# A 2D spectral filter and a 32-head attention on one core: earlier first tiles of x, fewer warming matmuls, a tail with narrow reciprocals, and other settings of the static order

## The chip, the core and the metric

The kernel runs on one core of a Trainium2 chip. The metric is the device time of one execution in microseconds (us). Several executions of a kernel are timed, each kernel beside the kernel before on the same chip; all executions quoted here were in the fast state. The profile is one of these executions, recorded. It has a "span", from its first to its last counted instruction, and the time of the same execution, which is somewhat longer. Two instants are used throughout: **F**, the start of the first softmax exponential on ScalarE, and **E**, the end of the last one. Head is what lies before F, tail what lies after E.

## The reference, cut to what matters

```python
def _A_ref(x, w_r, w_i):            # x: 1 x 2048 x 640
    X = rfft2(x.astype(float32)); X = X * (w_r + 1j * w_i)
    return irfft2(X, s=(2048, 640)).astype(bfloat16)
def _B_ref(x, wqkv, wo):            # 32 heads of 20, S = 2048, D = 640
    q, k, v = split_heads(x @ wqkv)
    p = softmax(q @ k.T * 20 ** -0.5)
    return merge_heads(p @ v) @ wo
return concatenate([a, b], axis=-1) # 1 x 2048 x 1280
```

Part A is computed with matmuls against Fourier matrices. Part B has 32 x 16 x 4 = 2048 score tiles of 128 x 512, each of which must be exponentiated.

## The kernel before: the parts concerned

The program is a generator. A scheduler runs on the host with estimated durations (`occupy`, `self.now`), decides which operation each engine does next and so writes one fixed order of instructions for each engine. The chip then follows these orders and waits only at semaphores. A change of an estimate or of a setting therefore changes the order for the whole run.

ScalarE exponentiates most score tiles, in groups of three and two PSUM banks; VectorE does 234 of the tiles with a polynomial.

```python
def try_exp(self):                                  # L1751
    ...
    self.P.add("act", lambda e: e.activation(pt, in_, AF.Exp, scale=SCALE, bias=-15.0 / LOG2E), ...)
    t = self.occupy("act", 512 * n * 0.8333 + 50.0, 0.0)
```

The head loads constants, then the first quarter of x (640 KB) as one transfer, all on SyncE's queue, and lets TensorE do 24 dummy matmuls to raise its clock.

```python
def setup_B(self):
    self.dma(self.ident, cBd.ap(), ...)
    self.dma(self.kq, kqd.ap(), ...)
    ldx(0); ldw(640, 736, "k0"); ldq(0, 96, 0); ldx(1); ldw(1280, 1360, "v0"); ldx(2); ldx(3)
    ...
    P.add("dve", lambda e: e.memset(ws, 0.25), ...)            # operand of the dummies
for i in range(cfg["WARMUP"]):                                 # 24
    self.dummy(i % 6)
```

The tail is the output projection of the last 512 rows. The row sums of the last unit are spread by a matmul to 128 x 512, inverted in four reciprocals of 128 x 128, and meanwhile TensorE does 28 pairs of output matmuls for the first seven head groups (`# ...` marks cuts).

```python
def tail_pe(self):
    ...
    self.P.add("pe", lambda e: e.matmul(ps[:, 5, :], sel, osb, start=True, stop=True), ...)   # L2040
    for qb in range(4):
        self.dve_urgent.append((self.tail_b, lambda qb=qb: self.tail_norm(qb)))
def tail_norm(self, qb):
    self.P.add("dve", lambda e: e.reciprocal(rb, b), ...)                                     # L2060
    self.P.add("dve", lambda e: e.tensor_tensor(o, osb, rb, ALU.mult), ...)
def tail_act(self):
    self.P.add("act", lambda e: e.copy(o[:, 0:512], ps[:, qb, :]), ...)                       # L2078
    self.P.add("act", lambda e: e.copy(o[:, 512:640], ps[:, 4, qb * 128:(qb + 1) * 128]), ...)
    self.P.add("sp", lambda e: e.dma_start(dst, o), ...)
```

The end of the program matters for what follows. A certificate is computed from the largest values met (reductions, three comparisons, a matmul that sums them, a comparison: `emit_flag`). Then every engine loads the verdict and branches over a second, slower program that would redo attention exactly.

```python
def run_engine(ename):
    def body(eng):
        fast.engine_body(fs, ename, eng)
        eng.wait_ge(fs["s_" + flag_task.eng], flag_task.count)     # wait for the verdict
        bad = eng.value_load(flag, min_val=0, max_val=3)
        with eng.If(bad > 0):
            ...
            slow.engine_body(ss, ename, eng)                       # a whole second program
        if ename == "sp": ...                                      # wait for the last stores
```

Of the kernel before, what the change touches and what calls it, by code (L numbers as in the profile page):

```python
# [10 lines left out]
BF16 = mybir.dt.bfloat16  # L11
U16 = mybir.dt.uint16
AF = mybir.ActivationFunctionType
# [1371 lines left out]
class FK(KB):  # L1385
# [8 lines left out]
    def alloc(self):  # L1394
# [21 lines left out]
        self.ws = a.bf(b0, 656)  # L1416
# [13 lines left out]
        self.ones1 = a.f32(take(32), 8)  # L1430
        self.zt = self.ones1.bitcast(BF16)[:, 8:9]
        self.sel = a.f32(take(512), 128)
# [3 lines left out]
    def zone(self, z, total):  # L1436
# [21 lines left out]
        self.ZT = a.bf(zC, 3 * 16 * 2 * 128).rearrange("p (t s c a) -> p t s c a", t=3, s=16, c=2)  # L1458
        self.yA = a.bf(zA, 16 * 640).rearrange("p (s d) -> p s d", s=16)
# [6 lines left out]
    def setup_B(self):  # L1466
        P = self.P
        cBd = self.inline(f32_to_bf16_bits(np.eye(128, dtype=np.float32)), "ident")
        self.dma(self.ident, cBd.ap(), w=[("ident",)], name="ld_ident")
# [5 lines left out]
        self.dma(self.kq, kqd.ap(), w=[("kq",)], name="ld_kq")  # L1475
# [3 lines left out]
        def ldx(i):  # L1479
            self.dma(self.xBn[:, 4 * i:4 * i + 4, :], xB[:, 4 * i:4 * i + 4, :], w=[("xBn", i)], name="ld_xB%d" % i)  # L1480
# [6 lines left out]
        ldx(0)  # L1487
        ldw(640, 736, "k0")
        ldq(0, 96, 0)
        ldx(1)  # L1490
        ldw(1280, 1360, "v0")
        ldx(2)
        ldx(3)
        ldw(736, 1280, "k")
        ldq(96, 640, 1)
        ldw(1360, 1920, "v")
        wq, ws, zt, va, ps, o1 = self.wq, self.ws, self.zt, self.Vaug, self.ps, self.ones1
        wo = self.wo_pad.rearrange("p g n -> p (g n)")
        P.add("dve", lambda e: e.memset(ws, 0.25), w=[("ws",), ("xa", 0)], name="ms_ws")
        P.add("act", lambda e: e.activation(ws[:, 640:648], ws[:, 0:8], AF.Exp), r=[("ws",), ("xa", 0)], w=[("ws2",)], name="act_warm")  # L1500
# [4 lines left out]
        P.add("dve", lambda e: e.memset(wo, 0.0), w=[("woz",)], name="ms_wo")  # L1505
# [9 lines left out]

    def load_wo(self):
        sel = np.zeros((128, 128), np.float32)
        for j in range(4):
            sel[32 * j + 20, 32 * j:32 * j + 32] = 1.0
        seld = self.nc.inline_tensor(sel, self.prefix + "sel")  # L1520
        self.dma(self.sel, seld.ap(), w=[("sel",)], name="ld_sel")
        wod = self.B_wo.rearrange("(g j d) n -> j d g n", g=8, j=4)
        for j in range(4):
            self.dma(self.wo_pad[32 * j:32 * j + 20, :, :], wod[j], r=[("woz",)], pw=[("wo",)], name="ld_wo%d" % j)
# [5 lines left out]
    def mk_jobs_B_static(self):  # L1530
        jobs = KB.mk_jobs_B_static(self)
        ps = self.ps
        for i in range(4):
            for gi in range(3):
                jobs[("xT", i, gi)].minp = (8000.0, 9500.0, 11500.0, 13000.0)[i]
        for g in range(NG):
            for kc in range(4):
# [16 lines left out]
                J.pe = pe  # L1554

# [3 lines left out]
                J.ev = [(mkev, 490.0, 600.0, [("kq",)], [("KT", g, kc)], [])]  # L1559
                J.mode = "c"  # L1560
                if g:
                    J.minp = 18500.0 + 1100.0 * g
        V = {}
        for part, h0, nh, per in ((0, 0, 4, 4), (1, 4, 4, 4), (2, 8, 12, 2), (3, 20, 12, 2)):
            n = 20 * nh
            for k0 in range(0, 16, per):
# [17 lines left out]
                J = Job("V%d_%d" % (k0, part), 0.0, pe, ev, after=[jobs[("xT", k0 // 4, gi)] for gi in range(3)], minp=19000.0 if part else 12000.0)  # L1584
# [8 lines left out]
    def dummy(self, bank, n=512):  # L1593
        ps = self.ps
        l = self.ws[:, 0:128]
        r_ = self.ident if n == 128 else self.ws[:, 128:128 + n]
        self.P.add("pe", lambda e: e.matmul(ps[:, bank, 0:n], l, r_, start=True, stop=True),
                   r=[("ws",), ("xa", 0)], w=[("ps", bank)], name="dummy")
# [19 lines left out]
    def job_QA(self, u):  # L1618
# [16 lines left out]
        def mkev(bank):  # L1635
            o = self.QA[u % 2]
            return lambda e, en: self.add_row(e, en, o, ps[:, bank, :], 2)
        ev = [(mkev, 490.0, 600.0, [("kq",)], [("QA", u % 2)], [])]
        cond = (lambda p: self.qk_left[u - 2] == 0) if u >= 2 else None
        J = Job("QA%d" % u, 0.0, pe, ev, after=[self.sj[("xT", qc, gi)] for gi in range(3)], cond=cond,  # L1640
                minp=(0.0 if u == 0 else 21000.0))
# [20 lines left out]
    def pe_dur(self, dur, mode, tiles=0):  # L1662
# [9 lines left out]
        if self.now < 12000.0:  # L1672
            dur *= 2.0
# [68 lines left out]
    def try_exp(self):  # L1742
# [10 lines left out]
        t = self.occupy("act", 512 * n * 0.8333 + 50.0, 0.0)  # L1753
# [221 lines left out]
    def unit_norm(self, u):  # L1975
# [7 lines left out]
        if u == 30:  # L1983
            self.tail_op = [(qb, g) for qb in range(4) for g in range(NG - 1)]
# [36 lines left out]
    def tail_mm(self, qb, g):  # L2021
        ps = self.ps
        l = self.OTn[:, g, qb * 128:(qb + 1) * 128]
        w1, w2 = self.wo_pad[:, g, 0:512], self.wo_pad[:, g, 512:640]

        def fn(e):
            e.matmul(ps[:, qb, :], l, w1, start=(g == 0), stop=(g == NG - 1))
            return e.matmul(ps[:, 4, qb * 128:(qb + 1) * 128], l, w2, start=(g == 0 and qb == 0), stop=(g == NG - 1),
                            skip_group_check=True)
        okey = ("OT", g) if g < NG - 1 else ("OTl", qb)  # L2030
        first = {"w": [("ps", qb)] + ([("ps", 4)] if qb == 0 else []), "pw": ([("ps", 4)] if qb else [])} if g == 0 else {"pw": [("ps", qb), ("ps", 4)]}
        self.P.add("pe", fn, r=[okey, ("wo",), ("woz",)], name="tail_op", **first)
        return self.occupy("pe", self.pe_dur(270.0, "f"), PE_LAT)

    def tail_pe(self):
        if not self.all_exp() or max(self.half_free) > self.now:
            return False
        if self.tail_t is not None and self.tail_t <= self.now and self.tail_b is None:
            ps, sel, osb = self.ps, self.sel, self.osb
            self.P.add("pe", lambda e: e.matmul(ps[:, 5, :], sel, osb, start=True, stop=True), r=[("osb",), ("sel",)], w=[("ps", 5)], name="tail_sum")  # L2040
            self.tail_b = self.occupy("pe", self.pe_dur(860.0, "f"), PE_LAT)
            for qb in range(4):
                self.dve_urgent.append((self.tail_b, lambda qb=qb: self.tail_norm(qb)))
            return True
        if self.tail_op:
            qb, g = self.tail_op.pop(0)
            self.tail_mm(qb, g)
            return True
        for qb in range(4):
            if self.tail_n.get(qb, 1e18) <= self.now:  # L2050
                del self.tail_n[qb]
                t = self.tail_mm(qb, NG - 1)
                self.tail_ev.append((t, qb))
                return True
        return False

    def tail_norm(self, qb):
        c = slice(qb * 128, (qb + 1) * 128)
        rb, b, osb, o = self.rb[:, c], self.ps[:, 5, c], self.osb[:, c], self.OTn[:, NG - 1, c]
        self.P.add("dve", lambda e: e.reciprocal(rb, b), r=[("ps", 5)], **({"w": [("rb",)]} if qb == 0 else {"pw": [("rb",)]}), name="tail_rec")  # L2060
        self.occupy("dve", 860.0)
        self.P.add("dve", lambda e: e.tensor_tensor(o, osb, rb, ALU.mult), r=[("osb",), ("rb",)], w=[("OTl", qb)], pw=[("OT", NG - 1)], name="tail_nrm")
        self.now += 950.0
        t = self.occupy("dve", 200.0, 100.0)
        self.now -= 950.0
        self.tail_n[qb] = t
        if qb == 3:
# [172 lines left out]
    def run(self):  # L2240
# [63 lines left out]
        for i in range(cfg["WARMUP"]):  # L2304
            self.dummy(i % 6)
# [100 lines left out]
```

## Time and profile before

| | before |
|---|---|
| time, median of the three runs before the prediction | 867.69 us (864.01 to 867.72) |
| profiled run | 866.46 us, span 862.5 |
| F, E | 15.36, 845.53 |
| exponentials busy on ScalarE | 823.3 |
| tail | 17.0 |

The prediction below shows the page, the head, the stretches and most of the tail. Two views are added here. The first is the list of ScalarE's waits; its columns are who waits, for whom, us in total, how often, and the longest.

```profile
ACT arena L1751 <- PE ps L1734: 6.6, 14, 1.1
```

So ScalarE waits in the middle only for score matmuls, and never longer than 1.1 us. The second is the end of the tail's timeline; its columns are start and duration in us, engine, line and operation.

```profile
855.69 2.73 SPq L2082 DMA_DIRECT2D out_dram<-arena  x4
...
856.78 0.14 DVE L2350 TENSOR_SCALAR arena<-arena 1x1 int32<-1x1 f32 x1
```

The last vector instruction (856.78) writes the verdict, the four stores have all been issued by 858.4, and the span goes on to 862.5. The distance from the verdict to the end, 5.6 us, is what the prediction did not look at closely enough.

### The profile page before, as it was taken

The page shows a single profiled execution, that of the slowest core. Times are in us where ns is not written, and L with a number is a line of the kernel's source. Part 1 is how long each engine was busy: PE and PEld are TensorE (multiplying, and loading weights), DVE is VectorE, ACT ScalarE, POOL GpSimd, SP SyncE. Part 2 cuts the span into 40 slices and gives each one's busy share as a digit, 9 for nine tenths or more (in the row PEclk, how much of TensorE's full clock was granted, in tenths as well). Part 3 has the DMA queues.
Part 4 walks back from the last instruction along what each step waited for, and adds up shares of the span by engine and source line. Part 5 has one row for each costly group of instructions (what it writes and reads, how often), then busy time and mean ns, then how long its engine had stood idle before and what let it go on. Part 6 is the DMA issues. An engine that isn't in the chain of part 4 may idle for free.

```text
span 862.5 us, 18266 instructions
## 1 busy us (share of the span) xinstructions
PE 791.6 (92%) x7750; PEld 274.6 (32%) x7783; DVE 764.9 (89%) x1472; ACT 832.0 (96%) x741; POOL 2.9 (0%) x7
## 2 busy tenths in 40 slices
PE   8999999999899899998889998888889999999986
PEld 4433323323323323332223332222333333332322
DVE  3387699999997999999999799999999889999973
ACT  5999999999999999999999999999999999999993
POOL 1000000000000000000000000000000000000000
PEclk9999999999999999999999999999999999999999
DMA  7440000000321000001101000001002111002211
GB/s 243 91 89 14 2 14 15 14 14 8 96 88 44 15 14 14 3 16 48 50 14 38 22 3 12 14 14 29 24 13 63 37 34 32 7 14 67 76 44 34
DMA packets 34268, 31.96 MB, mean 37 GB/s; under 512 B 13700, under 2 KB 28292, under 8 KB 34180
## 3 DMA queue, kind: packets, MB, share of 16 engines
q1 hardware_dynamic: 34180, 30.73, 12.2%
q8 instruction: 62, 1.02, 0.5%
q14 instruction: 26, 0.21, 0.1%
HBM read 24.97 MB, written 5.50 MB: 35 GB/s over the span
## 4 chain that ended last, share of the span: by engine, by line
ACT 57%; DVE 29%; PE 12%; issue 1%; ACTq 0%; DVEq 0%
ACT arena L1751 57%; DVE arena L1825 5%; DVE arena L227 5%; PE ps L1734 3%; DVE arena L1253 3%; DVE arena L1514 3%; DVE arena L1865 2%; DVE arena L1872 2%; DVE arena L1869 2%; PE ps L1920 2%; DVE arena L2203 1%; DVE arena L1863 1%; PE ps L1548 1%; DVE arena L1861 1%; DVE arena L1867 1%; PE ps L2000 1%
## 5 line engine op out<-in xcount | busy, mean ns | idle before, releaser
L1751 ACT ACTIVATE arena<-ps 128x1536 bf16<-128x1536 f32 x726 | 823.3, 1365 | 7.4 <-PE ps L1734 6.6
L1734 PE MATMUL ps<-arena 32*128 32x512 bf16 x2048 | 313.0, 384 | 45.3 <-ACT arena L1751 29.1
L1920 PE MATMUL ps<-arena 128*32 128x512 bf16 (+3 forms) x2048 | 188.4, 385 | 2.5 <-ACT arena L1751 0.9
L1825 DVE TENSOR_SCALAR arena<-ps 128x512 uint16<-128x512 f32 x234 | 159.3, 684 | 10.7 <-PE ps L1734 9.9
L1734 PEld LDWEIGHTS ps<-arena 32*128 32x128 bf16 x2048 | 77.6, 91 | 285.9 <-ACT arena L1751 211.6
L227 DVE CAST arena<-ps 128x320 bf16<-128x320 f32 (+3 forms) x190 | 103.9, 547 | 27.2 <-PE ps L1576 13.9
L1865 DVE TENSOR_TENSOR arena<-arena 128x1024 f16<-128x1024 uint16 x117 | 80.2, 686 | 1.2
L1869 DVE TENSOR_TENSOR arena<-arena 128x1024 f16<-128x1024 f16 x117 | 80.4, 688 | 0.6
L1872 DVE TENSOR_TENSOR arena<-arena 128x1024 uint16<-128x1024 uint16 x117 | 79.9, 684 | 0.4
L1614 PE MATMUL ps<-arena 128*32 128x512 bf16 x760 | 72.8, 387 | 0.5 <-DVE arena L1940 0.5
L1514 DVE TENSOR_SCALAR arena<-ps,arena 128x512 bf16<-128x512 f32 x62 | 50.0, 806 | 23.0 <-PE ps L1548 16.2
L1920 PEld LDWEIGHTS ps<-arena 128*32 128x32 bf16 (+1 forms) x2048 | 46.0, 93 | 70.5 <-issue 57.2
L1548 PE MATMUL ps<-arena 128*32 128x512 bf16 x640 | 52.8, 384 | 0.8 <-ACT arena L226 0.3
L1861 DVE TENSOR_SCALAR arena<-arena 128x1024 uint16<-128x1024 uint16 x117 | 49.3, 422 | 0.8
L1863 DVE TENSOR_SCALAR arena<-arena 128x1024 f16<-128x1024 uint16 x117 | 49.2, 421 | 0.9
L1630 PE MATMUL ps<-arena 128*32 128x512 bf16 x640 | 49.3, 382 | 0.4 <-DVE arena L227 0.3
L1867 DVE TENSOR_SCALAR arena<-arena 128x1024 f16<-128x1024 uint16 x117 | 49.0, 419 | 0.4
L227 DVE COPY arena<-ps 128x1024 bf16<-128x1024 bf16 (+2 forms) x55 | 40.1, 731 | 9.1 <-PE ps L540 7.9
L1334 PE MATMUL ps<-arena 128*128 128x320 bf16 (+1 forms) x192 | 36.4, 302 | 0.0
L2000 PE MATMUL ps<-arena 128*128 128x320 bf16 x192 | 35.8, 302 | 0.0
L1170 PE MATMUL ps<-arena 128*128 128x328 bf16 x160 | 31.6, 306 | 0.7 <-DVE arena L227 0.7
L1576 PE MATMUL ps<-arena 128*128 128x80 bf16 (+1 forms) x320 | 31.2, 236 | 0.0
(69 smaller groups left out, 424.4 us busy)
## 6 DMA issues: line engine op xcount, KB each, us to landing
arena<-rscr SPq DMA_DIRECT2D x31, 256.0 KB
arena<-in_B_x_dram SPq DMA_DIRECT2D x4, 640.0 KB, 6.3
arena<-in_A_x_dram SPq DMA_DIRECT2D x4, 640.0 KB, 5.0
out_dram<-arena SPq DMA_DIRECT2D x16, 160.0 KB, 1.8
out_dram<-arena SPq DMA_DIRECT2D x4, 640.0 KB, 3.3
arena<-f_ciCS SPq DMA_DIRECT2D x8, 256.0 KB, 3.0
arena<-arena SPq DMA_DIRECT2D x124, 2.0 KB, 1.7
arena<-f_cslab SPq DMA_DIRECT2D x2, 768.0 KB, 4.4
```

The costliest lines, as they stand in the source:

```text
L227: return eng.tensor_copy(out, in_)
L1514: return e.tensor_scalar(out, in_, m, b, ALU.mult, ALU.add)
L1548: inst = e.matmul(ps[32 * j:32 * j + 32, bank, :], self.wqkv[:, cbv, c:c + 32], r_, start=st, stop=sp, tile_position=(0, 32 * j))
L1614: i = e.matmul(ps[32 * j:32 * j + 32, 6, :], z, k, start=False, stop=False, skip_group_check=True, tile_position=(0, 32 * j))
L1734: inst = e.matmul(ps[:, bank, :], kt_[32 * j:32 * j + 32, g, kt * 128:(kt + 1) * 128], q[32 * j:32 * j + 32, :], start=True, stop=True, ti ...
L1751: self.P.add("act", lambda e: e.activation(pt, in_, AF.Exp, scale=SCALE, bias=-15.0 / LOG2E), r=[("ps", h + k) for k in range(n)], w=[("PT ...
L1825: self.P.add("dve", lambda e: e.tensor_scalar(v, in_, 1024.0 * SCALE * LOG2E, 31743.0, ALU.mult, ALU.min), r=[("ps", bank)], **({"w": [key ...
L1861: t = self.x_op(n, one, lambda e: e.tensor_single_scalar(sh, v, 6, ALU.logical_shift_left), [kv], [ka], "x_s")
L1865: t = self.x_op(n, two, lambda e: e.tensor_tensor(b16, sh, b16, ALU.mult), [ka, kb], [kb], "x_q")
L1869: t = self.x_op(n, two, lambda e: e.tensor_tensor(b16, b16, a16, ALU.mult), [ka, kb], [kb], "x_h")
L1872: t = self.x_op(n, two, lambda e: e.tensor_tensor(v, v, b16, ALU.add), [kb, kv], [kv], "x_w")
L1920: inst = e.matmul(ps[32 * j:32 * j + m, 6, :], va[:, kt, 21 * h:21 * h + m], pt, start=st, stop=sp, tile_position=(0, 32 * j))
```

## The change

Its intent: start the exponentials earlier, take the wide reciprocals out of the tail, and settle the middle with other settings. The core of the diff; cuts are marked with `...`.

```diff
 def setup_B(self):
+    P.add("pool", lambda e: e.memset(o1b, 1.0), ...)              # one column feeds the dummies
-    self.dma(self.ident, cBd.ap(), ...); self.dma(self.kq, kqd.ap(), ...)
-    ldx(0)
+    P.add("act", lambda e: e.dma_start(ident, src), ...)
+    ldx0(0, "sp"); ldx0(2, "act"); ldx0(1, "sp"); ldx0(3, "act")  # 4 x 160 KB, two queues
     ldw(640, 736, "k0"); ldq(0, 96, 0)
-    ldx(1)
+    ldx(1, [("xBn", 0, 1), ("xBn", 0, 3)])                        # waits for pieces 1 and 3
 ...
+    for tt in range(4):                                           # transposes by 128 rows
+        jobs[("xT", 0, tt)] = Job("xT0_%d" % tt, ...)
-    J.ev = [(mkev, 490.0, 600.0, ...)]                            # estimates of evictions
+    J.ev = [(mkev, 740.0, 717.0, ...)]
 ...
-    t = self.occupy("act", 512 * n * 0.8333 + 50.0, 0.0)
+    t = self.occupy("act", 512 * n * 0.8333 + 64.0, 0.0)
 ...
+def tail_jobs(self):                  # last 256 rows, first 7 head groups: summed before the tail
 ...
+    for qb in range(4):               # sums turned: 128 rows x 4 columns per block
+        i = e.matmul(ps[:, 2, 4 * qb:4 * qb + 4], osb[:, qb * 128:(qb + 1) * 128], selT, ...)
 ...
+def tail_rec(self):
+    P.add("dve", lambda e: e.reciprocal(rc, rin), ...)            # 16 columns
+    for h in range(2): P.add("dve", lambda e, ...: e.tensor_copy(o, in_), ...)
 ...
+    self.P.add("pe", lambda e: e.matmul(o, l, idf, ...), name="tail_spread")   # turned back
+def tail_add(self, qb, half): ... e.tensor_tensor(o, a, b, ALU.add)            # + the early sums
+    self.P.add("act" if qb == 3 else "sp", lambda e: e.dma_start(dst, o), ...)
 ...
-    cfg=dict(..., T_A=600000.0, PVQ=6, WIN=1400.0, ALONE=0.0, PVB=12, PTB=5)
+    cfg=dict(..., T_A=760000.0, PVQ=12, WIN=1000.0, ALONE=1200.0, PVB=10, PTB=6, WARMUP=10)
```

T_A spreads part A over time; PVQ, PVB and PTB rule when value products are taken up and in how large batches; WIN is the window in which the scheduler counts TensorE's load; ALONE holds back score tiles that VectorE is to do.

## The prediction

> **What bounds the kernel now.** I read the page first, for which engine is full. Each group line gives source line, engine, operation, shapes, count; then busy us and mean ns; then idle us before them and what ended it.
>
> ```profile
> PE 791.6 (92%) x7750; PEld 274.6 (32%) x7783; DVE 764.9 (89%) x1472; ACT 832.0 (96%) x741; POOL 2.9 (0%) x7
> ...
> L1751 ACT ACTIVATE arena<-ps 128x1536 bf16<-128x1536 f32 x726 | 823.3, 1365 | 7.4 <-PE ps L1734 6.6
> ```
>
> ScalarE is the bound: 726 exponentials fill 823.3 of 862.5 us, with only 7.4 us of idle before them. The span is therefore head + exponentials + holes + tail. The timeline of the first 33 us and the chain of waits in that stretch give the head (start us, us, engine, line):
>
> ```profile
> 0.73 1.28 ACT L1500 ACT_TABLE_LOAD   x1 [0.73 <-PEq L2391]
> 1.60 0.51 SPq L362 DMA_DIRECT2D arena<-in_B_x_dram  x1
> 1.61 8.05 PE L1597 MATMUL ps<-arena 128*128 128x512 bf16 x24 [1.61 <-DVE arena L1499]
> 7.13 2.04 PEld L1597 LDWEIGHTS ps<-arena 128*128 128x128 bf16 x10 [0.27 <-issue]
> 9.50 1.73 PE L540 MATMUL ps<-arena 128*128 128x128 bf16 x28
> 10.15 2.84 ACT L226 COPY arena<-ps 128x1024 bf16<-128x1024 bf16 x3 [7.91 <-PE ps L540]
> 12.13 0.83 PE L1548 MATMUL ps<-arena 128*32 128x512 bf16 x12 [0.30 <-ACT arena L226]
> 14.09 0.78 ACT L1513 ACTIVATE arena<-ps,arena 128x512 bf16<-128x512 f32 x1 [0.30 <-PE ps L1630]
> 15.36 17.27 ACT L1751 ACTIVATE arena<-ps 128x1536 bf16<-128x1536 f32 x15 [0.49 <-PE ps L1734]
> ```
>
> The reader is to see that the first exponential starts at 15.36, and that what holds it is not x (its first 640 KB are in by about 6.4 us, by the packets and the landing records) but 24 dummy matmuls, which keep TensorE until 9.66. From 15.36 the next 15 exponentials run without a hole.
>
> The middle: busy time by stretch of the run. The columns are the stretch, its length, then busy us and count of PE, PEld, DVE, ACT, POOL, then clock, DMA share, GB/s.
>
> ```profile
> 15.36:845.53 830.17, 768.20 (x7569) 263.13 (x7599) 753.41 (x1448) 823.27 (x726) 0.29 (x1) 1.00 0.11 33
> 845.53:862.50 16.97, 10.20 (x70) 5.37 (x72) 7.70 (x18) 2.83 (x8) 0.00 (x0) 0.94 0.13 42
> ```
>
> So 830.2 us from the first exponential to the last, of which 6.9 idle, and a tail of 17.0. The tail, from the timeline:
>
> ```profile
> 846.03 0.69 DVE L1940 COPY arena<-ps 128x512 f32<-128x512 f32 x1 [9.01 <-PE ps L1920]
> 847.01 1.08 PE L2040 MATMUL ps<-arena 128*128 128x512 f32 x2
> 848.12 0.96 DVE L2060 RECIPROCAL arena<-ps 128x128 f32<-128x128 f32 x1 [1.40 <-PE ps L2040]
> 853.07 0.29 DVE L2062 TENSOR_TENSOR arena<-arena 128x128 bf16<-128x128 f32 x1
> 854.91 0.58 ACT L2078 CAST arena<-ps 128x512 bf16<-128x512 f32 x1 [9.39 <-PE ps L2028]
> 857.75 0.31 ACT L2079 CAST arena<-ps 128x128 bf16<-128x128 f32 x1
> ```
>
> Two things run side by side until about 854: four reciprocals of 128 columns on VectorE (848.12 to 853.36) and 28 pairs of output matmuls on TensorE at about 0.27 us a pair (846 to 854). ScalarE waits 9.39 us for the latter. After the last cast (858.06) come the store and the end, 4.4 us.
>
> **What the Trainium skill says.** "TensorE: Matmul & The Clock Gate", Part 1, has the array at half clock until a whole activity window of about 3.4 us was busy; the window is free-running, and cold matmuls are N/1.2 ns apart. The trace agrees: the weight loads of the dummies come 0.43 us apart (512/1.2) until 7.1 us, then 0.20 apart. TensorE began at 1.61, so warming took 5.5 us, as if the first window, only partly busy, did not count. "ScalarE: Activation LUTs", What ACT_TABLE_LOAD costs, gives 0.833 ns a column plus 186 less 93 of overlap, 93 ns an instruction. Here 1814 tiles of 512 columns at 426.7 ns make 774.0 us, so the 726 instructions cost (823.3 - 774.0)/726 = 68 ns each; I use 68. "DMA: Bandwidth & Descriptors", Anatomy of one DMA, has about 2 us fixed whatever the size. The page shows 1.8 us to landing for 32 KB, 1.8 for a 160 KB store and 6.3 for a 640 KB load of x, in a stretch at some 350 GB/s. "Trainium Kernel Development and Optimization", Key Constraints: several issuing queues share the same 16 DMA engines and save only issue time. Here one issue of x takes 0.51 us, so that is what the second queue saves, once or twice.
>
> **The change part by part.** The built order of both programs gives the counts.
>
> Head. Gone: memset of the dummies' operand (0.60 on VectorE), 14 of 24 dummies, constants ahead of x. Dummies can now start at about 0.9 (GpSimd's memset starts at 0.73, 0.1 long). Ten cold ones are 10 x 0.427 = 4.3, done at 5.2. The four pieces of x, issued from 0.73, should start to move at 1.7 as the 32 KB constant did, 672 KB at 350 GB/s end at 3.6, and land by 4.2: before the dummies end. Then 20 transposes at 0.062 = 1.25, latency 0.2, one copy of 640 columns at about 0.7 (1.02 for 1024), 0.1 of semaphores: K starts at 7.45. From there to the first exponential, with before's durations: 40 matmuls at 0.054 plus latency 2.35, the second eviction 0.8, scores and wait 0.5: 3.65. First exponential at **11.1**, against 15.36: 4.3 us earlier. But the second quarter of x now waits for the first pieces, so it lands no earlier than before (about 8.5), and the order has ScalarE evict one K tile after six exponentials (15 tiles, 15 x 0.427 + 6 x 0.068 = 6.8 us), then scores: TensorE gets to that K only after the sixth group's scores, 4.5 us in, and does 0.4 + 0.45 + 0.45 + 0.22 + 0.65, then ScalarE 0.8 and scores 0.45. I charge a **1.2 us** hole that before did not have. Net -3.1.
>
> Exponentials. ScalarE has 362 of three tiles, 363 of two, none of one (before 363, 362, 1); VectorE 236 tiles for 234. Change: -(1280+68) + (853+68) - (427+68) ns = **-0.9**.
>
> Middle. Before lost 6.9 us less the 0.5 counted at the first group: 6.4, in 13 waits for scores. New queue settings, eviction estimates nearer the trace (740 and 717 ns against a measured 777 and 806) and part A spread to 760 instead of 600 us should cut some; 204 + 13 more dummy matmuls (about 14 us of TensorE at 0.216 a row of four) can add some. I choose 5.0: **-1.4**.
>
> Tail. From the last exponential's end E (845.53 before): value product and copy end at E+1.2 as before; the four sum matmuls have 4 columns but load float32 weights, twice each by the two records at L2040 with 0.15 to 0.2 a load: 8 x 0.2, so E+3.0. VectorE: maximum 0.15, reciprocal of 16 columns 0.25 (measured elsewhere on the page), two spreading copies 0.35: E+4.4, against E+7.8 before. But the order has TensorE run 29 output matmuls between sums and spreading: 29 x 0.135 = 3.9, to E+6.9. Four float32 spreading matmuls at 0.35: E+8.3. Normalise and multiply the last block: E+9.1. VectorE's four additions at 0.48: E+10.9, against E+12.5 before. The certificate chain (three reductions, three comparisons, a matmul, two more, about 1.3 us as before) now stands behind the additions at E+12.2 and may outlast the store. So the tail is about **15.5** instead of 17.0: -1.5. TensorE, not the reciprocals, keeps most of what was to be won.
>
> Sum: -3.1 - 0.9 - 1.4 - 1.5 = -6.9 us.
>
> **The rivals.** (1) The clock does not warm: with the window placed badly, or broken by the wait for copies after the transposes, K and Q run cold, +2.3 us, and the transposes +0.9. For it: 5.5 us to warm before, and only 10 dummies. It would make 863. (2) The middle turns worse: TensorE and VectorE are at 92 and 89% and get more to do, and a static order that drifts from the chip makes holes. For it: the stretch 600 to 700 had five such waits; against it, 700 to 845 had none at similar load. Ten us of holes would make 865. (3) The middle is what improves: all holes gone, and the tail runs as intended with the spreading ahead (13.5): 853.5. (4) Pure head and tail without the hole: 859.
>
> **Range and chances.** Median before 867.69 less 6.9 gives 860.8; the profiled run (866.46 for a span of 862.5, so 4.0 above its span) gives 862.5 - 6.9 + 4.0 = 859.6. I take 860.0. The range 854.5 to 865.5 spans rivals 1 to 4; the three runs before already differ by 3.7. Two per cent is 17.4 us; head, holes and half the tail together would have to vanish for that. Faster 0.03, same 0.95, slower 0.02.
>
> **What would show it.** First exponential at 10.5 to 12; dummies ending near 5.2 and before x has landed; a K eviction on ScalarE after six exponentials with 1 to 2 us of hole; exponentials busy 822.4; waits of ScalarE for scores of 3 to 7 us; from the last exponential to the end 14.5 to 16.5, TensorE in output matmuls when VectorE's spreading copies are done. Wrong if scores are late by over 10 us in the middle, or K and Q run at half clock.

## The result and the profile after

The changed kernel took **861.41 us** (median of four runs, 861.24 to 861.87), beside 867.12 us (864.01 to 867.72) of the kernel before in the same rounds. The ratio is 0.9942, with a 95% interval of 0.9917 to 0.9967. A ratio here and below is the mean time of one kernel's fast runs over that of the other's fast runs of the same rounds, so it is not quite the ratio of the medians. The profiled run took 861.56 us for a span of 859.8, at a mean granted clock of 0.995 (before 0.999).

From the page after, the row of the engines and the group of the exponentials (busy us and mean ns, then idle us before them and what ended most of it):

```profile
PE 809.8 (94%) x8000; PEld 281.2 (33%) x8000; DVE 765.2 (89%) x1485; ACT 830.1 (97%) x738; POOL 2.9 (0%) x8
...
L1783 ACT ACTIVATE arena<-ps 128x1536 bf16<-128x1536 f32 x725 | 822.8, 1355 | 7.4 <-PE ps L1766 6.8
```

ScalarE is still the bound, at 97%. The exponentials are one fewer and 0.5 us shorter in all, and the idle time ahead of them has not gone down. The stretches from the end of the new hole in the head to E, and from E to the end; columns as in the prediction:

```profile
19.46:841.70 822.24, 784.04 (x7737) 266.55 (x7736) 754.41 (x1453) 815.86 (x719) 0.29 (x1) 1.00 0.10 32
841.70:859.80 18.10, 9.39 (x68) 6.20 (x66) 5.18 (x21) 2.27 (x7) 0.00 (x0) 0.86 0.12 41
```

The tail became longer: 18.1 us, before 17.0. The head's timeline:

```profile
0.89 4.26 PE L1629 MATMUL ps<-arena 128*128 128x512 bf16 x10 [0.89 <-POOL arena L1471]
...
4.99 1.32 PE L1558 MATMUL ps<-arena 128*128 128x128 bf16 x20
...
6.89 1.26 PE L1581 MATMUL ps<-arena 128*32 128x512 bf16 x20 [0.58 <-DVE arena L227]
...
10.56 6.89 ACT L1783 ACTIVATE arena<-ps 128x1536 bf16<-128x1536 f32 x6 [0.49 <-PE ps L1766]
...
18.19 0.78 ACT L1524 ACTIVATE arena<-ps,arena 128x512 bf16<-128x512 f32 x1 [0.74 <-PE ps L1581]
...
19.46 26.33 ACT L1783 ACTIVATE arena<-ps 128x1536 bf16<-128x1536 f32 x23 [0.49 <-PE ps L1766]
```

Ten dummies end at 5.15, transposes start at once at 4.99 (ends of matmuls are modelled, so the two overlap a little), K matmuls at 6.89, and the first exponential at 10.56. But after six exponentials, at 17.45, ScalarE stops; it evicts a K tile at 18.19 and exponentiates again only at 19.46. The tail's timeline:

```profile
844.32 0.25 DVE L2146 RECIPROCAL arena<-arena 128x16 f32<-128x16 f32 x1
...
844.74 3.98 PE L2084 MATMUL ps<-arena 128*128 128x320 bf16 x28 [0.52 <-ACT arena L226]
...
848.56 0.61 PE L2123 MATMUL ps<-arena 128*128 128x128 f32 x4
...
851.63 1.69 DVE L2170 TENSOR_TENSOR arena<-ps,arena 128x320 bf16<-128x320 f32 x4 [0.21 <-PE ps L2084]
...
853.35 0.35 ACTq L2181 DMA_DIRECT2D out_dram<-arena  x1
...
854.22 0.14 DVE L2462 TENSOR_SCALAR arena<-arena 1x1 int32<-1x1 f32 x1
```

The reciprocal of 16 columns takes 0.25 us, and then TensorE is in output matmuls from 844.74 until the first spreading matmul starts at 848.56. The last store is issued at 853.35 and landed at 855.29. The verdict is written at 854.36. The span goes on to 859.76.

Why it goes on is told by records that the page doesn't count as busy (loads of the verdict, branches, drains). Read from the trace, in us:

```
                                     before    after
E                                    845.53   841.70
verdict written                      856.92   854.36
TensorE's branch starts              857.83   855.27
   and takes                           4.34     4.13
other engines' branches take, each   0.05 to 0.07 (after)
last store landed                    861.8    855.29
last instruction ends                862.52   859.76
verdict to end                         5.60     5.40
```

Before, the last store landed at 861.8 and TensorE's branch ended at 862.2, side by side. After, the store had landed 4.5 us before the end: TensorE's branch alone holds the end. The branch records of the other engines are short, but after them ScalarE, VectorE and GpSimd came to their next instruction only 2.6 to 3.3 us later (0.13 to 0.16 us in experiment 3, where the second program is left out), so these engines are held up too, only less than TensorE. The Trainium skill, "Runtime: NRT & Kernel Launch", Instruction fetch mechanics, says that a taken branch whose target lies outside the window of fetched instructions waits for a transfer of them. The trace agrees in kind, and an experiment below measures it: the branch goes over the whole second program.

The sum of the difference, all from the two profiled runs (866.46 to 861.56):

| part | before | after | change | predicted |
|---|---|---|---|---|
| F | 15.36 | 10.56 | -4.80 | -4.3 |
| hole after the sixth exponential | 0 | 2.01 | +2.01 | +1.2 |
| exponentials busy | 823.27 | 822.76 | -0.51 | -0.9 |
| other holes between F and E | 6.90 | 6.38 | -0.52 | -1.4 |
| tail | 16.99 | 18.05 | +1.06 | -1.5 |
| time of the run beyond its span | 3.94 | 1.80 | -2.14 | 0 |
| sum | | | -4.90 | -6.9 |

### The profile page after: what moved, and what is told of

Same layout as the page of the kernel before. It is cut to its first block, busy times and chain, and to the rows that moved or that the text cites. A ratio compares the mean times of both kernels' runs of the same rounds, so it can differ in the third digit from the quotient of the medians.

```text
span 859.8 us, 18764 instructions
## 1 busy us (share of the span) xinstructions
PE 809.8 (94%) x8000; PEld 281.2 (33%) x8000; DVE 765.2 (89%) x1485; ACT 830.1 (97%) x738; POOL 2.9 (0%) x8
## 4 chain that ended last, share of the span: by engine, by line
ACT 58%; DVE 26%; PE 15%; issue 1%; DVEq 0%; POOL 0%; POOLq 0%
ACT arena L1783 57%; DVE arena L227 6%; DVE arena L1857 4%; PE ps L1766 4%; DVE arena L1253 3%; PE ps L2032 2%; PE ps L1952 2%; DVE arena L1897 2%; DVE arena L1901 2%; DVE arena L1904 2%; PE ps L1581 1%; DVE arena L1895 1%; DVE arena L1899 1%; DVE arena L1893 1%; PE ps L1662 1%
## 5 line engine op out<-in xcount | busy, mean ns | idle before, releaser
L1766 PE MATMUL ps<-arena 32*128 32x512 bf16 x2048 | 309.8, 385 | 26.8 <-ACT arena L1783 14.4
L1952 PE MATMUL ps<-arena 128*32 128x512 bf16 (+3 forms) x2048 | 190.5, 386 | 0.8 <-DVE arena L227 0.4
L1857 DVE TENSOR_SCALAR arena<-ps 128x512 uint16<-128x512 f32 x236 | 162.1, 688 | 13.3 <-PE ps L1766 12.2
L1646 PE MATMUL ps<-arena 128*32 128x512 bf16 x964 | 89.6, 389 | 1.6 <-DVE arena L1972 1.4
L1952 PEld LDWEIGHTS ps<-arena 128*32 128x32 bf16 (+1 forms) x2048 | 46.1, 93 | 74.3 <-issue 61.3
L227 DVE COPY arena<-ps 128x1024 bf16<-128x1024 bf16 (+4 forms) x59 | 42.4, 721 | 19.3 <-PE ps L540 7.7
L1581 PE MATMUL ps<-arena 128*32 128x512 bf16 x640 | 51.0, 383 | 0.7 <-DVE arena L227 0.6
L1662 PE MATMUL ps<-arena 128*32 128x512 bf16 x640 | 49.3, 382 | 0.4 <-DVE arena L227 0.3
L1646 PEld LDWEIGHTS ps<-arena 128*32 128x32 bf16 x964 | 23.2, 94 | 47.2 <-issue 38.9
L1334 PE MATMUL ps<-arena 128*128 128x320 bf16 (+1 forms) x192 | 38.3, 303 | 0.1
```

Source lines behind the costliest of these rows:

```text
L227: return eng.tensor_copy(out, in_)
L1581: inst = e.matmul(ps[32 * j:32 * j + 32, bank, :], self.wqkv[:, cbv, c:c + 32], r_, start=st, stop=sp, tile_position=(0, 32 * j))
L1646: i = e.matmul(ps[32 * j:32 * j + 32, 6, :], z, k, start=False, stop=False, skip_group_check=True, tile_position=(0, 32 * j))
L1766: inst = e.matmul(ps[:, bank, :], kt_[32 * j:32 * j + 32, g, kt * 128:(kt + 1) * 128], q[32 * j:32 * j + 32, :], start=True, stop=True, ti ...
L1857: self.P.add("dve", lambda e: e.tensor_scalar(v, in_, 1024.0 * SCALE * LOG2E, 31743.0, ALU.mult, ALU.min), r=[("ps", bank)], **({"w": [key ...
L1952: inst = e.matmul(ps[32 * j:32 * j + m, 6, :], va[:, kt, 21 * h:21 * h + m], pt, start=st, stop=sp, tile_position=(0, 32 * j))
```

## The experiments

Twelve kernels ran. Those of one group ran on the same chip and share the runs of the kernel before, whose medians were 865.44 (first four), 865.79 (next four) and 866.12 us (last four). The theory after the result: the tail grew because the verdict and the branch after it are its path, not the sums or the store; the hole at 17.4 comes from TensorE's order; the new settings are worth little. Rivals: the tail is longer through the sums and the store; the hole comes from x arriving late; the settings are what improved the middle.

### 1. The new head and settings with the whole old tail

```diff
-    def tail_jobs(self): ...  tail_mm, tail_pe, tail_rec, tail_norm, tail_add, tail_store, tail_act (new)
+    def tail_mm(self, qb, g): ...  tail_pe, tail_norm, tail_act (those of before)
-            self.tail_jobs()
+            self.tail_op = [(qb, g) for qb in range(4) for g in range(NG - 1)]
```

> The changed kernel with the whole tail of the kernel before (order identical up to the last few us). Theory: the new tail is the longer one, because its certificate verdict comes 12.7 us after the last exponential against 11.4, so undoing it takes the stretch from the last exponential to the end from 18.1 to about 17.0 us and the time down by about 1.1 us (860.3). Rival, the step of the prediction: the new tail saves 1.5 us, so undoing it costs 1.5 us (862.9).

Measured: 859.93 us (859.55 to 860.11), ratio to before 0.9936 (0.9919 to 0.9952), span 858.3, tail 16.88. The new tail thus costs 1.2 us of span in the tail alone (18.05 against 16.88), and 1.2 us of time against the changed order on the same chip (861.14, experiment 4), or 1.5 against 861.41. This refutes the prediction's step that it saves 1.5. TensorE's branch took 4.19 us here, the last store landed at 857.72, and the end came at 858.30.

### 2. The certificate's work moved ahead in the new tail

```diff
+        self.flag_dve()     # reductions and comparisons right after the spreading copies
...
+                if qb == 0:
+                    self.flag_pe()   # the summing matmul ahead of the first spreading one, bank 6
...
-        self.emit_flag()    # at the very end
```

> The changed kernel with the certificate chain ahead of the normalisation, in time that VectorE spends waiting (verdict about 7.5 us after the last exponential instead of 12.7). Theory: the end is the verdict plus 5.4 us, of which TensorE's branch over the second path is 4.1 us; with the verdict early, TensorE branches when its last output matmul is done (10.5 us after the last exponential), so the tail is about 16 us and the time 2 us lower (859.3). Rival: the last store's landing sets the end, so nothing changes (861.4).

Measured: 859.28 us (859.15 to 859.66), ratio 0.9929 (0.9912 to 0.9946), span 857.8, tail 16.26. The timeline of this kernel's tail, its verdict and its last store:

```profile
848.89 0.14 DVE L2467 TENSOR_SCALAR arena<-arena 1x1 int32<-1x1 f32 x1
...
853.50 0.35 ACTq L2183 DMA_DIRECT2D out_dram<-arena  x1
```

The verdict is now written (849.03) 4.5 us before the last store is issued, and it no longer decides. But the tail falls by only 1.8 us, because each engine still branches after its own last work: TensorE's branch starts at 852.88 and takes 3.93 us, and ScalarE, which issues the last store, branches at 854.79 and comes to its next instruction only at 857.49, just before the end. This version is the best here that keeps the fallback and whose runs agree: the changed kernel's order, run on the same chip in experiment 4, took 860.80 to 861.48, and no run of the one reaches the range of the other.

### 3. The second program left out

```diff
                     eng.nop().then_inc(join, 1)
-                    eng.wait_ge(join, 5)
-                    slow.engine_body(ss, ename, eng)
-                    if ename == "sp":
-                        for sname in slow_streams: ...
```

> The changed kernel with the body of the second path left out, so that the branch over it is short (the result is the same, the path is never taken). Theory: the 4.1 us branch is the cost of jumping over that path; without it the end comes 1 to 2 us after the verdict, limited by the store: tail 14 to 15 us, time 3 to 4 us lower (858). Rival: the branch waits for something else, such as the store: tail stays at 18.1.

Measured: 857.69 us (857.44 to 857.72), ratio 0.991 (0.9894 to 0.9927), span 855.9, tail 14.47. The result was correct on these inputs, but the kernel gives up its fallback, so it is a measurement and no candidate. Nothing else differs from the changed kernel, and TensorE's branch fell from 4.13 to 0.23 us:

```
                          after    second program left out
TensorE's branch takes     4.13       0.23
verdict to end             5.40       1.8
tail                      18.05      14.47
```

So 3.6 us of the tail are the price of branching over a long program, in every execution that never takes the other path.

### 4. The second quarter of x not made to wait

```diff
-        ldx(1, [("xBn", 0, 1), ("xBn", 0, 3)])
+        ldx(1)
```

> The changed kernel without the wait of the second quarter of x for the first pieces; all orders are the same. The second quarter should land about 2 us earlier (8.5 instead of 10.5). Theory: the 2.0 us hole of ScalarE at 17.5 comes from TensorE's static order (K stands behind the sixth group's scores and transposes of the third quarter), so it stays at 1.8 to 2.0. Rival: it comes from the late landing, so it falls below 1 us. The first exponential may be up to 0.5 us later, as the pieces share the transfer rate.

Measured: 861.14 us (860.80 to 861.48), ratio 0.9951, span 859.4. The order of instructions is the same. The quarter had landed by 9.22 instead of 10.18, so 1.0 us earlier and not 2. ScalarE's timeline shows the eviction of the K tile and the exponential after it:

```profile
19.13 0.78 ACT L1524 ACTIVATE arena<-ps,arena 128x512 bf16<-128x512 f32 x1 [0.74 <-PE ps L1581]
20.40 1.45 ACT L1783 ACTIVATE arena<-ps 128x1536 bf16<-128x1536 f32 x1 [0.49 <-PE ps L1766]
```

In this run the six exponentials before end at 18.38, so the hole is 2.02 us, as before. The hole doesn't come from x; K matmuls come late in TensorE's static order, and ScalarE waits 0.74 us for them, then needs the eviction and the scores.

### 5. The kernel before with ten dummies

```diff
-    ... PVB=12, PTB=5))
+    ... PVB=12, PTB=5, WARMUP=10))
```

> The kernel before with 10 dummy matmuls instead of 24, nothing else; all orders after them are the same. Theory, step of the prediction: the dummies, not x, hold the head, so TensorE goes from dummies (end about 5.9) to transposes when x lands at 6.2, the first exponential comes at 12.3 to 13.3 instead of 15.4, and the last exponential ends 2 to 3 us earlier. Rival 1: the clock is then cold for K and Q, first exponential at 14 or later. Rival 2: the gain is given back in the middle by later waits (last exponential moves by less than 1 us). Beside it: the stretch between the last instruction and the end of the timed run, 3.4 to 4.1 us in all runs of before and 1.8 of the changed one, would become 1.8 if it hangs on the length of TensorE's program.

Measured: 863.84 us (861.92 to 866.15, twelve runs), ratio 0.9978 (0.9966 to 0.9990). TensorE's timeline in the head:

```profile
1.61 4.45 PE L1597 MATMUL ps<-arena 128*128 128x512 bf16 x10 [1.61 <-DVE arena L1499]
...
9.29 0.62 PE L540 MATMUL ps<-arena 128*128 128x128 bf16 x8 [1.27 <-DMA arena<-in_B_x_dram]
```

The dummies end at 6.06, but the order puts eight transposes of the second quarter of x ahead of K, and these waited 1.27 us for its landing. F is 13.51, somewhat later than expected; E is 843.54, 2.0 us earlier than before. In this profile fewer dummies alone are worth part of the head's gain; the other part needs the smaller first pieces and the order that goes with them. But the profile is one of the fastest of the twelve runs. Their median span is 862.0 us, the same as that of before in this group, so the whole median gain of 1.95 us lies beyond the span. Five runs with a mean clock of 0.998 or more have spans of 860.1 to 860.9 (before at such clocks: 861.3 to 862.2); the other seven, at 0.991 to 0.997, have 861.8 to 864.4. So the gain in the head is seen only in the runs whose clock stayed up. Why the clock is lower in more runs than before (7 of 12, against 13 of 32) is not shown. In all twelve runs the time beyond the span was 1.8 to 1.9 us, where before has 3.2 to 4.2. These two programs differ only in 14 dummy matmuls, so it hangs on TensorE's program and not on its tail or its stores.

### 6. The changed kernel with 24 dummies

```diff
-    ... PTB=6, WARMUP=10))
+    ... PTB=6, WARMUP=24))
```

> The changed kernel with 24 dummies instead of 10. Theory: dummies end at 7.9 to 9.0, first exponential at 13.8 to 14.9 (from 10.5 to 11.5), so the last exponential ends about 3.3 us later and the time is about 864.5. Rival: the pieces of x alone bring the head's gain and the dummies hide under the loading: under 1 us. The stretch after the last instruction stays at 1.8 if TensorE's program length does not matter.

Measured: 863.32 us (863.22 to 863.96, nine runs), ratio 0.9968. TensorE's dummies:

```profile
0.90 7.68 PE L1629 MATMUL ps<-arena 128*128 128x512 bf16 x24 [0.90 <-POOL arena L1471]
```

They end at 8.58; F is 13.95 and E is 843.99, 2.3 us later than in the changed kernel. The time is 1.9 us longer, less than the 3.4 us by which F moved. Part of it lies in the clock: the profiled run of the changed kernel had half a clock for 3.4 us near 230 us (shown further down), and this run had not. Against the runs of experiments 2 to 4, which had no such drop either (F at 11.4 to 11.5, E at 841.4 to 841.5), both F and E moved by 2.5 us. What the dummies delay in the head is delayed to the end; the rival, that the dummies hide under the loading, is refuted.

### 7. The changed kernel with the old settings

```diff
-    ... T_A=760000.0, PVQ=12, WIN=1000.0, ALONE=1200.0, PVB=10, PTB=6, WARMUP=10
+    ... T_A=600000.0, PVQ=6, WIN=1400.0, ALONE=0.0, PVB=12, PTB=5, WARMUP=10
```

> The changed kernel with the queue settings and the pace of part A of the kernel before (10 dummies kept). Prediction: the settings cut the holes by some of its 1.4 us. Theory now: holes after the first 20 us were 6.3 us under both settings, so nothing changes beyond 1.5 us either way, though the filler matmuls (964 rows of four's quarters, against 760) fall and the half-clock stretch at 230 us goes. Rival: the settings are needed with the new head, and without them holes grow by over 3 us.

Measured: 869.90 us (869.03 to 872.0, six runs), ratio 1.0051 (1.0035 to 1.0067), span 867.2. The theory, that the settings are worth under 1.5 us, fell: they are worth 8.5. F is 10.68, as good as unchanged, and E is 850.23. ScalarE's waits:

```profile
ACT arena L1783 <- PE ps L1766: 8.9, 12, 1.9
...
ACT arena L1783 <- PE ps L1952: 6.2, 4, 2.2
```

The holes between F and E are 16.2 us, with 7.3 of them between 500 and 600 us. A new kind of wait has come, 6.2 us for value products (L1952): a group of exponentials waits for the buffer of an older one, which no value product has yet read.

### 8. The hole at 17.4 shut by another order

```diff
-                jobs[("xT", i, gi)].minp = (0.0, 9500.0, 11500.0, 15500.0)[i]
+                jobs[("xT", i, gi)].minp = (0.0, 9500.0, 13500.0, 15500.0)[i]
+                if g == 0 and kc in (1, 2, 3):
+                    J.ev_eng = "dve"          # first K tiles evicted by VectorE
```

> The changed kernel with the transposes of the third quarter of x held back in the order so that the second K tile comes before them, and that K tile evicted by VectorE instead of ScalarE. Theory: the 2.0 us hole of ScalarE after six exponentials (0.7 waiting for K, 0.8 eviction, 0.5 scores) falls to about 0.5 to 1, and the time by about 1 us (860.3), if no later hole takes its place. Rival: the hole moves to the third K tile at about 25 us and nothing is gained.

Measured: 868.29 us (867.66 to 869.02, fourteen runs), ratio 1.0028 (1.0019 to 1.0036), span 864.6. ScalarE's timeline:

```profile
17.88 6.88 ACT L1785 ACTIVATE arena<-ps 128x1536 bf16<-128x1536 f32 x6 [0.52 <-PE ps L1768]
25.37 0.43 ACT L226 CAST arena<-ps 128x320 bf16<-128x320 f32 x1 [0.61 <-PE ps L1612]
26.51 1.01 ACT L226 COPY arena<-ps 128x1024 bf16<-128x1024 bf16 x1 [0.71 <-PE ps L540]
27.42 13.67 ACT L1785 ACTIVATE arena<-ps 128x1536 bf16<-128x1536 f32 x12
```

The hole at 17.4 fell from 2.01 to 0.52 us, as meant. But the scheduler then gave ScalarE two other evictions at 25.37 and 26.51, which opened one of 2.66 us, and further holes came at 165 (1.9) and 594 (2.3): 13.3 us in all. Of the 6.9 us by which this kernel is slower than the changed one, 2 lie beyond its span, which the time exceeds by 3.5 to 4.3 us as in the kernel before. What was shut in one place came back in others, as the rival said, though not at a K tile.

### 9. The certificate early and the spreading matmuls ahead

```diff
 def tail_pe(self):
+        for qb in range(4):
+            if self.tail_n.get(("e", qb), 1e18) <= self.now: ...    # spreading first
+                bk = (4, 3, 2, 4)[qb]                               # banks of their own
         if self.tail_op: ...                                        # then output matmuls
```

> The changed kernel with the certificate ahead (as in a_flag) and the four spreading matmuls ahead of 26 of the 28 output matmuls, in three PSUM banks instead of one, so that they neither stand behind 3.9 us of TensorE work nor wait for each other's normalisation. Theory: TensorE's total work in the tail stays, only the waits between spreading matmuls (2 x 0.4 us) and the chain behind them shorten; tail 15.3 to 15.7 us against 16.3 in a_flag and 18.1, time about 858.4. Rival: TensorE is the bound to the end anyway, so nothing over a_flag (859.3).

Measured: 860.10 us (858.69 to 860.88, five runs), ratio 0.9923 (0.9909 to 0.9937). The five runs fall into two groups, 858.7 to 858.9 and 860.1 to 860.9. The profile fell in the longer group, with a tail of 17.80. Two stretches of it, with columns as before (the clock is the third number from the end):

```profile
843.35:846.76 3.41, 2.27 (x17) 1.54 (x17) 2.56 (x15) 0.42 (x1) 0.00 (x0) 1.00 0.02 5
846.76:850.17 3.41, 3.41 (x15) 1.91 (x14) 0.29 (x2) 0.00 (x0) 0.00 (x0) 0.50 0.02 5
```

The clock was halved from 846.76 to 850.17. The 34 output matmuls that begin at 846.70 took 6.66 us; at the full clock the same number would take about 4.8 (an estimate: 34 x 0.142, from 28 in 3.98). In the window before, TensorE had been busy 2.27 of 3.41 us. Its longest waits there were for VectorE's comparisons ahead of the certificate's matmul and for a copy of ScalarE (0.52 us), not between the spreading matmuls, which run on end for 1.36 us:

```profile
845.39 0.19 PE L2466 MATMUL ps<-arena 128*1 128x3 f32 x2 [0.62 <-DVE arena L2460]
845.51 1.36 PE L2099 MATMUL ps<-arena 128*128 128x128 f32 x8
```

The expected 858.4 is nearly reached by two runs of five; neither was profiled, so it is not shown that they escaped the half clock. Keeping the clock up with dummies there was not tried.

### 10. The spread of part A alone set back

```diff
-    ... T_A=760000.0, ...
+    ... T_A=600000.0, ...
```

> The changed kernel with one setting undone: the pace of part A, finished by 600 instead of 760 us. Undoing all settings cost 8.5 us, of which 7.3 us of holes between 500 and 600 us. Theory: the pace is the cause (part A's evictions crowd VectorE there), so the holes between 500 and 600 us return, 4 us or more, and the time is 866 or more. Rival: the settings for the value products are the cause, and this run stays within 2 us of 861.4.

Measured: 861.06 us (860.73 to 861.98), ratio 0.9943, span 859.1. This was a wasted variant: the built order is instruction for instruction that of the changed kernel, which a comparison of the two orders would have shown ahead of the run. The setting is inert here, so it explains nothing of the 8.5 us. As a repeat on another chip run it confirms 861.4.

### 11. The settings of the value products alone set back

```diff
-    ... PVQ=12, ... PVB=10, PTB=6, ...
+    ... PVQ=6, ... PVB=12, PTB=5, ...
```

> The changed kernel with the three settings for the value products undone (6, 12, 5 instead of 12, 10, 6); pace and fillers new. Theory (pace is the cause): within 2 us of 861.4. Rival: ScalarE waits for probability buffers behind value products, as at 540 us with all settings undone (6.2 us of waits for value products), so 4 us or more are lost, 866 or more.

Measured: 865.47 us (864.88 to 866.31, twenty runs), ratio 0.9991 (0.9984 to 0.9997), span 863.4; E is 845.23 and the holes are 12.1 us. ScalarE's longest hole:

```profile
516.05 4.62 ACT L1783 ACTIVATE arena<-ps 128x1536 bf16<-128x1536 f32 x4 [3.24 <-PE ps L1952]
```

One wait of 3.24 us for a value product, of the kind that all the old settings together brought, though theirs came later, at 540 to 575 us. These three settings are worth 4.1 us of the 8.5. The others, WIN and ALONE, or their interplay with these, have the rest; no run tells them apart.

### 12. The kernel before with the new settings

```diff
-    ... T_A=600000.0, PVQ=6, WIN=1400.0, ALONE=0.0, PVB=12, PTB=5
+    ... T_A=760000.0, PVQ=12, WIN=1000.0, ALONE=1200.0, PVB=10, PTB=6
```

> The kernel before with the new settings only (old head, old tail, old estimates of durations; 24 dummies). If the settings are good in themselves, the holes after the first exponential fall from 6.9 to about 3 us and the time by some 4 us. If they fit only the new order, holes stay or grow: 865 to 872. Its exponentials are one of three tiles and two of two fewer; -3.2 us if two more VectorE tiles' worth holds.

Measured: 870.31 us (869.26 to 871.36), ratio 1.0050 (1.0034 to 1.0066), span 867.5; the holes are 17.2 us, 7.6 of them between 33 and 100 us. Its time beyond the span is 1.8 us, so the span alone (median 868.45 against 862.3) lost 6 us. So the new settings are not better in themselves. Each set goes with its own program, and on the other one it costs 4 to 9 us of time:

| holes between F and E, us | old settings | new settings |
|---|---|---|
| program before | 6.9 | 17.2 |
| program after | 16.2 | 8.4 |

## Why the prediction was right or wrong

The predicted 860.0 us lay 1.4 us below the measured median, and within 2% as foreseen. That the sum came out is partly luck: the tail was 2.6 us worse than predicted (+1.06 against -1.5), and 2.14 us after the span vanished, which was not forecast. Without the second the time would have been some 863.6 (an estimate: 861.41 + 2.14). So the steps are judged singly.

**What bounds the kernel: right.** ScalarE stayed the bound. In the profiled runs of experiments 5 and 6 what moved F moved E as well, apart from the clock's part told below; over all runs of experiment 5 the median span did not fall.

**The head: right in mechanism, near in size.** F was 11.1 by the prediction and 10.56 as measured; the dummies ended at 5.15 against 5.2. But the last piece of x landed at 5.81 and not at 4.2: the estimate let x alone use the queue's 350 GB/s, while the engines moved some 260 GB/s in that stretch and weights were issued from 1.67 on. The transposes go piece by piece, so this cost nothing. The text also put the landing "before the dummies end" in one place and after their end in another; it was after. K began at 6.89 instead of 7.45, since the copies of the transposed pieces were shared by ScalarE and VectorE and ran beside the transposes.

**The hole: foreseen, too small.** It was 1.2 us by the prediction and 2.01 in fact. The eviction and the scores were as reckoned; the step that failed is "TensorE gets to that K only after the sixth group's scores, 4.5 us in". These scores started at 15.84, 5.3 us in, and ScalarE waited 0.74 us. The second quarter of x, too, landed later than reckoned, at 10.18 and not at about 8.5 (9.06 in before), but experiment 4 shows that its wait has no part in the hole.

**Exponentials and middle: right in sign, too large for this profile.** The exponentials have -0.5 against -0.9, and the other holes -0.5 against -1.4. Other profiles of the same middle (experiments 1 to 4, 9 and 10) have 822.05 to 822.21 us of exponentials, so -1.1 to -1.2, and those without a drop of the clock 5.95 us of other holes, so -0.9; the sizes are those of one run. Here the working had a slip: 830.17 less 823.27 is 6.90 and already free of the 0.5 us ahead of F, which was then taken off once more. Its 5.0 us is to be held against 6.38. One hole of 0.45 us among these, at 231.8, falls in a stretch of half clock from 230.11 to 233.52. The prediction gave the settings little weight ("should cut some"). They carry far more: with the old ones on the new order the time is 8.5 us longer (experiment 7), with the new ones on the old order 4.2 (experiment 12). The small net of the middle is a fit between settings and order.

**The tail: wrong in sign.** The prediction had -1.5 and the profile has +1.06. Its walk through the tail was close for as long as it went:

| after E, us | predicted | measured |
|---|---|---|
| value product and copy end | 1.2 | 1.3 |
| sums done | 3.0 | 2.4 |
| spreading copies done | 4.4 | 3.4 |
| output matmuls done | 6.9 | 7.0 |
| additions done | 10.9 | 11.6 |
| verdict written | 12.2 | 12.66 |
| end | 15.5 | 18.05 |

The mis-sized term is the last: 3.3 us after the verdict, where both kernels take 5.4 to 5.6. The prediction said that the certificate chain "may outlast the store", but charged it as if what followed were a store's end. The working should have taken the distance from verdict to end from the profile before, where verdict at 856.78 and end at 862.5 stood on the same view. In before the verdict came 11.4 us after E and the store's way was about as long, so the certificate hid beside the store; the change moved it behind the additions, 1.27 us later, while shortening only what was beside it. Experiments 1, 2 and 3 confirm this from three sides. The remark that TensorE, not the reciprocals, keeps most of what was to be won is right as a reading of the order (28 matmuls ahead of the spreading) but was not what set the end; in the profile of experiment 9, with both repaired, half a clock took an estimated 1.8 us (6.66 against 4.8).

**What was not foreseen: 2.14 us after the span.** The prediction added a constant 4.0 us to the span. It is 3.2 to 4.3 in all runs of before and of experiment 8, and 1.8 to 1.9 in all others, experiment 5 among them, which is the kernel before less 14 dummies. In the trace, after the last instruction, before has a gap of 2.03 us (from 863.63) in the resets of semaphores that close the program, and experiment 8 one of 2.10; none of the twelve other profiles has one. Near it a packet of 16,384 bytes comes on the instruction queue, at 863.32. But such a packet comes near the end of the others too (except experiment 3), 0.80 us after the last instruction in before and 0.76 in after, so its time does not tell them apart. What in TensorE's program makes the gap stays open.

**The rivals.** Rival 1 (a cold clock) did not happen to the full: K and Q ran at the full clock in the profiled run, where it rose at 4.83. In other runs of the same order (experiments 10 and 4) it rose at 5.78 and 6.86; F was then 0.4 and 0.9 later, and E was not. The middle shows where the gain went: in the three profiles of this order in which the clock rose earliest (by 4.83), it was also halved once near 230 us. The windows of the profiled run:

```profile
226.70:230.11 3.41, 2.24 (x26) 0.58 (x23) 3.08 (x5) 3.41 (x4) 0.00 (x0) 1.00 0.01 1
230.11:233.52 3.41, 3.41 (x29) 0.75 (x31) 0.90 (x2) 2.96 (x3) 0.00 (x0) 0.50 0.25 56
```

TensorE was busy 2.24 of 3.41 us in the first and lost half its clock in the second; runs with a later clock have their windows elsewhere and no drop. Busy time alone does not decide it: before was busy 2.08 us in its window from 525.94 to 529.35 and kept the full clock. What does is open. From F to E the four profiled runs without a drop (experiments 2, 3, 4 and 10) take 830.0 to 830.1 us, the three with one (the changed kernel, experiments 1 and 9) 831.0 to 831.1. So the early clock gave back in the middle what it won in the head. Rival 2 (a worse middle) did not happen in the change as made, and did in four variants (experiments 7, 8, 11 and 12), by 4 to 10 us of holes. Rival 3 needed a tail of 13.5, and the shortest profiled with the fallback kept is 16.26. Rival 4 needed a head without the hole, which was there with 2.01 us.

## What to carry to other kernels

Walk the tail to the very last instruction, branches and drains included, and ask of each thing that is moved what was hidden beside it: here a shorter chain of sums lost to a verdict of a few small instructions that came 1.3 us later. In a statically ordered program a setting that helps with one order can hurt with another (experiments 7 and 12), so a change of order and its settings must be judged together, and built orders compared before anything runs. A fallback behind a branch cost 3.6 us here in every execution, and raising the decision ahead of the last work won back 1.8 of them. A profile is one execution: hold it against the spans and clocks of all runs, as experiment 5 shows.

## What the Trainium skill lacked or had wrong

- "TensorE: Matmul & The Clock Gate", Part 1, puts the warming at about 4 us of matmuls, give or take 0.5. With the same ten dummies from 0.9 us on, the clock rose between 3.66 and 6.86 us, so 2.8 to 6.0 us after the first matmul. The page's free-running window, and its own remark that the number of slow matmuls varies from run to run, agree with this spread; its 0.5 does not.
- The same section lets the clock fall after an idle window, and in a subsection after frequent short pauses, without a measure for them. Here it was halved after windows in which TensorE was busy 2.24 and 2.27 of 3.41 us, and not after one with 2.08 (before, from 525.94).
- "Runtime: NRT & Kernel Launch", Instruction fetch mechanics, has the wait of a taken far branch but no duration. TensorE's took 3.9 to 4.4 us over the second program and 0.23 us when that was left out; the end moved by 3.6 us.
- No page has the 2.1 us after the last instruction which come and go with TensorE's program (time beyond the span 3.2 to 4.3 against 1.8 to 1.9).
- "ScalarE: Activation LUTs", What ACT_TABLE_LOAD costs, leaves 93 ns an instruction beside the columns; 726 exponentials of two and three banks show 68 ns.
- "DMA: Bandwidth & Descriptors", Anatomy of one DMA, has a fixed time, but for transfers issued by GpSimd; for those issued by SyncE and ScalarE, as here, the page has the time to the first byte and no such fit. A store of 160 KB alone took 1.8 us to landing, and 160 KB pieces of x issued beside one another 2.7 and 3.6 us.
